# A linear-attention and feed-forward kernel: two prefetched weight pieces and eight small loads of the opening are put behind a GpSimd copy

## The chip, the core and the metric

The kernel runs on one core of one Trainium2 chip. Its time is the device time of one launch in microseconds (us). Three runs of the kernel before gave 631.48, 631.27 and 630.54 us, with a median of 631.27 us.

The core has five engines that work side by side, each through its own list of instructions in order: TensorE (PE in the profile; its weight loads are shown apart as PEld), VectorE (DVE), ScalarE (ACT), GpSimd (POOL) and SyncE (SP). SP computes nothing here. It issues DMA transfers from DRAM into the on-chip memory, one after the other, and an instruction of SP that has to wait holds up every transfer behind it.

## What is computed

The first half is a delta rule, a linear attention with a state that is corrected step by step, for 4 batches of 8 heads, 768 positions and 48 dimensions a head. The second half is a feed-forward layer with a leaky ReLU whose slope differs from unit to unit, on 3072 tokens of 384 features, with 2048 hidden units.

```python
k_n = k / (norm(k) + 1e-6)
for t in range(768):
    y[t]  = q[t] @ state
    v_old = state.T @ k_n[t]
    state = state + beta[t] * outer(k_n[t], v[t] - v_old)
x = y as (tokens, 8 heads * 48)
h = x @ w_in
g = max(h, 0) + alpha * min(h, 0)
out = g @ w_out
```

## The kernel before, in words

The sequence is cut into 12 chunks of 64 positions, and a chunk into two steps of two batches each, so there are 24 steps, numbered from 0. Steps 0 and 1 are the first chunk. Within a chunk the recurrence is a triangular system, and a step solves it with small matmuls: three rounds of substitution (lines 719 to 757), and then `solve` (line 907), whose result, `u`, VectorE takes out of PSUM with one instruction (line 914). From `u` come the step's outputs (line 923), and the state for the next chunk (line 942). Two steps make one chunk of 256 tokens for the feed-forward layer.

All instructions stand in the order in which the Python code emits them; no scheduler moves them. While the attention is a chain of small dependent matmuls, feed-forward matmuls (line 1088) are woven between them so that TensorE has work. The opening has no such work yet: `first_chunk` (line 1630) runs the three rounds for steps 0 and 1 in turn (line 732), with transposes of keys 4, 5 and 6 between them (line 430), then the two solves, the outputs, and the first feed-forward input (`to_ffn`). After it `second_pair` (line 1857) does steps 2 and 3 with the first feed-forward matmuls between.

The weights of the first layer, `w_in`, come in 12 pieces of 512 KB. A piece is fetched by one DMA into a staging place (line 246), rewritten there by two ScalarE instructions (lines 262 and 263, the function `begin`), and finished by two VectorE instructions (lines 272 and 277, the function `finish`). Pieces 0 to 5 and 8 to 11 are staged in the place that `w_out` will take later. Pieces 6 and 7 are staged in `space_out` (the trace names them by that tile). `spare_words` is a view of that tile, and the gates `beta` lie in its first words until they have been transposed. In ScalarE's list the two instructions for piece 6 and the two for piece 7 stand right behind the two copies of `to_ffn` for the first chunk (line 993), and ahead of the first ReLU of the feed-forward layer (line 1098).

Queries, keys and values come as 96 KB transfers (line 169), two to a step, each of 512 rows of 192 bytes, and the keys once more in another layout, as `kl`, in four transfers of 48 KB a step (line 197). These go through SP, in the order in which the code calls `load_early`, `load_q`, `load_v`, `load_late` and `fetch_in`. Eight semaphores are used for them in turn, so a transfer is issued only once the transfer eight places before it has landed.

In the opening SP's order is: keys, `beta`, values and queries of the first steps, weight pieces 0 to 5, then

```
weight pieces 6 and 7            fetch_in(n_in + 2), n_in = 6
keys 4, 5, 6                     load_early
kl of step 1                     load_late(1)
values 2, queries 2, queries 3   load_v, load_q
key 7                            load_early(NJ + NKE), NJ + NKE = 7
weight pieces 8 and 9            fetch_in(n_in + 4)
kl of step 2, values 3, ...      second_pair
```

Key 7 takes the place of key 4, and queries 2 and 3 those of queries 0 and 1, so they wait for the transposes of these; pieces 8 and 9 take the places of pieces 0 and 2 once VectorE has finished with them.

Of the kernel before, what the change touches and what calls it, by code (L numbers as in the profile page):

```python
# [25 lines left out]
FP32 = mybir.dt.float32  # L26
# [18 lines left out]
def kernel(  # L45
# [11 lines left out]
    nc = tc.nc  # L57
# [24 lines left out]
    def ps_one():  # L82
        return ps_big()[:, 0]
# [21 lines left out]
    def half(i):  # L105
        return slice(64 * i, 64 * i + 64)
# [17 lines left out]
    NKE, NKL, NQ = 3, 2, 2  # L124
# [11 lines left out]
    def early(n):  # L136

        if n >= TURNED_K:
            return k_last
        return k_late[1] if n == NKE else k_early[n % NKE]  # L140

    def fetch_blocks(src, c, first, dst):

        src = src.rearrange("b (g a) s d -> a (b g) s d", a=2)
        n = dst.shape[2]
        for i in range(2):
            at = c * C + HB * i
            for a in range(2):
                for e in range(2):
                    w = min(HB, D - HB * e)  # L150
                    x = src[a, first : first + n, at : at + HB, HB * e : HB * e + w]
                    rows = slice(64 * a + HB * e, 64 * a + HB * e + HB)
                    nc.sync.dma_start(
                        out=dst[rows, i, :, 0:w], in_=x.rearrange("x s d -> s x d")
                    )

    def blocks_of(x):
        return x.rearrange("p (i x e) -> p i x e", i=2, e=HB)
# [6 lines left out]
    def fetch(a, n, dst, queues=(nc.sync, nc.sync)):  # L165
        c, bp = steps[n]
        for t in range(2):
            src = a[2 * bp + t, :, c * C : (c + 1) * C, :].rearrange("h p d -> p h d")
            queues[t].dma_start(out=dst[half(t)], in_=src)

    def load_early(n, *queues):
        if n < N:
            fetch(k, n, early(n)[:, :, 0:D], *queues)

    def load_q(n):
        if TURNED_Q <= n < N:
            c, bp = steps[n]
            x = q_pad[n % NQ].rearrange("p h d -> p (h d)")
            fetch_blocks(q, c, 2 * bp * H // 2, blocks_of(x))
        elif n < N:  # L180
            fetch(q, n, q_pad[n % NQ][:, :, 0:D])

    def load_v(n):
        if n < N:
            v_raw[n] = work.tile([128, H, D], FP32, name="v_raw", bufs=3)
            fetch(v, n, v_raw[n])
# [113 lines left out]
    for t in range(2):  # L300
# [5 lines left out]
        out=ones, in_=ones, compare_op=ALU.is_ge, fill=1.0, base=0,  # L306
# [7 lines left out]
    for t in range(2):  # L314
# [5 lines left out]
        out=first_of, in_=ident.rearrange("p (q u e) -> p u q e", u=2, e=HB // 2)[:, 0],  # L320
# [162 lines left out]
    def quarters():  # L483
        return [(g, a, t) for g in range(G) for a in range(2) for t in range(2)]

    def now(pieces):
        for x in pieces:
            x()

    def region(p, n, **into):  # L490

        p = ps_big()[:, :, 0:n] if p is None else p
        assert p.shape[-1] == n
        return p.rearrange("p a (g i) -> p a g i", **into)
# [34 lines left out]
    NJ = 4  # L529
# [139 lines left out]
    def off_products(both):  # L669

        x = [act[:, FP - 4 + i].rearrange("p f i -> p (f i)") for i in both]
        x = [y.rearrange("p (h c) -> p h c", h=H) for y in x]
        for i in both:
            own = turned[0][:, i * H : i * H + H]
            nc.scalar.mul(x[i][:, :, 0:HB], own, which[:, 0:1])
            nc.vector.tensor_scalar_mul(x[i][:, :, HB:C], own, which[:, 1:2])
        n = C - LB
        own, other = [ps_big(), None], ps_big()
        own[1] = ps_big()
        for i in both:  # L680
            p = own[i][:, 0, 0 : H * n].rearrange("p (b i) -> p b i", b=H)
            q = (other[:, 0] if i == 0 else own[1][:, 1])[:, 0 : G * n]
            q = q.rearrange("p (b i) -> p b i", b=G)
            for b in range(H):
                for t in range(2):
                    w, y = x[i][half(t), b], mid[i][half(t), b, LB:C]
                    nc.tensor.matmul(p[half(t), b], w, y)
                    if b >= G:
                        nc.tensor.matmul(q[half(1 - t), b - G], w, y)
            nc.scalar.copy(diag[i][:, :, LB:C], p)  # L690
            other_.append(q)
        return [
            lambda i=i: nc.vector.tensor_copy(out=away[i][:, :, LB:C], in_=other_[i])
            for i in both
        ]
# [23 lines left out]
    def substitute(n, x, k, p=None):  # L719

        p = region(p, G * D, g=G)
        for g, a, t in quarters():
            frm, to, m, y = half(t), half(t), diag[n % NE][:, a * G + g], x[:, a, g]
            if a == 0:
                pass
            elif k % 2 == (1 if n < 2 else 0):
                to = half(1 - t)
            else:
                frm, m = half(1 - t), away[n % NE][:, g]
                if k == 0:  # L730
                    y = crossed[n][:, g]
            nc.tensor.matmul(p[to, a, g], m[frm], y[frm])
        return p
# [22 lines left out]
    def place_inverse(n):  # L756

        for i in range(2):
            nc.scalar.mul(
                inv[n % NE][:, :, HB * i : HB * i + HB], inverse[0][:, n * H : n * H + H],  # L760
                which[:, i : i + 1],
            )
# [88 lines left out]
    nv, rhs_, ys, us, xts, whole = {}, {}, {}, {}, {}, set()  # L851
# [55 lines left out]
    def solve(n, p=None):  # L907
        p = region(p, G * D, g=G)
        for g, a, t in quarters():
            nc.tensor.matmul(  # L910
                p[half(t ^ a), a, g], inv[n % NE][half(t), a * G + g], rhs_[n][half(t), a, g]
            )
        us[n] = work.tile([128, 2, G, D], FP32, name="u")
        return [lambda: nc.vector.tensor_tensor(  # L914
            out=us[n], in0=p,
            in1=stats[n][1][:, 0:3:2, :, None].to_broadcast([128, 2, G, D]), op=ALU.mult,
        )]
# [712 lines left out]
    def first_chunk(mask, inverted, convert):  # L1630

        both = (0, 1)
        ahead[0] = n_in
        aways = off_products(both)
        for _ in range(PIECES - 1):
            next(inverted)
        aways[0]()
        next(inverted)
        assert next(inverted, None) is None
        aways[1]()  # L1640
        place_inverse(0)
        now_at = {}
        for i in both:
            now_at[i] = rhs_[i]
        for k in range(3):
            for i in both:
                p = substitute(i, now_at[i], k)
                if k == 0:
                    now_at[i] = work.tile([128, 2, G, D], FP32, name="r")
                substituted(i, now_at[i], p, k)  # L1650
                if i == 0 and k < 2:
                    now(flipped(NJ + k, ps_one()))
                if (k, i) == (1, 0):
                    place_inverse(1)
                if (k, i) == (0, 1):
                    place(0, (3,))
                    for j in (3, 2):
                        off_blocks(j, by_pool=True)
                if (k, i) == (1, 1):
                    place(1, (3,))  # L1660
                    begin_in(6)
                if i == 0 and k > 0:
                    mask(0, k - 1)
        for i in both:
            squared(NJ + i)
        for i in both:
            rhs_[i] = now_at[i]
        weighted = solve(0)
        keys = flipped(NJ + 2, ps_one())
        now(weighted)  # L1670
        for a in range(2):
            mask(1, a)
        now(keys)
        now(solve(1))
        convert(6)
        for i in both:
            now(outputs(i))
        load_early(NJ + NKE)
        fetch_in(n_in + 4)
        for i in both:  # L1680
            to_ffn(i, ps_ffn())
        norms(NJ)
        ahead[0] = FT * DM
        convert(4)
        norms(NJ + 1)
# [26 lines left out]
    n_in = FT * DM // n  # L1712
    stages = [space[:, i * n : (i + 1) * n] for i in range(n_in)]
    spare_words = space_out.rearrange("p s e -> p (s e)")
    stages += [spare_words[:, i * n : (i + 1) * n] for i in range(2)]
    ids = [*range(n_in + 2), 0, 2, 1, 3]
    fetch_in, begin_in, conv_in = weights(pieces, stages, ids, in_done, n_in + 2)
# [89 lines left out]
    gram_3 = gram(3)  # L1807
    turned_beta = big[1]
    later_signs = betas(1, NCH // 2, turned_beta[:, 1, G * C :])
    fetch_in(n_in + 2)  # L1810
    cross(0)
    nc.scalar.copy(inside, ones)
    now(gram_2[2:])
# [3 lines left out]
    edges(0, edge)  # L1817
    cross(1)
    load_late(1)
    load_v(2)  # L1820
    for i in range(2):
        flips(N, i)
    for i in range(2):
        load_q(i + 2)
    mask = queries()
    for i in range(2):
        off_blocks(i)
# [15 lines left out]
    def convert(n):  # L1843
        for _ in part(conv_in, n):
            pass
# [294 lines left out]
```

## Time and profile before

| | |
|---|---|
| three runs, median | 631.27 us (630.54 to 631.48) |
| the profiled execution's own time | 632.44 us |
| its span, first to last instruction | 630.7 us |
| granted TensorE clock, mean | 0.997 |
| PE busy | 617.4 us, 98% of the span |
| DVE, ACT, POOL busy | 504.0, 312.4, 99.9 us |
| moved by DMA | 39.26 MB, mean 62 GB/s |

In the profile, a row of the timeline gives the start and the length in us, the engine, the source line, what the instruction writes and reads with its shape, and in brackets how long the engine had been idle before it, and what ended that. "<-issue" means that nothing the profile shows was waited for. A row of busy times by stretch gives, for the stretch named first, its length, then the busy time and the number of instructions of PE, PEld, DVE, ACT and POOL, the granted TensorE clock, the mean busy share of the 16 DMA engines, and GB/s. A row of DMA issues gives what is written and read, the queue, the number, the size of one in KB, and the median us from issue to landing. Rows of DMA queues give packets, MB, and busy time as a share of 16 engines' time; the queue "q8 instruction" carries program code, not data.

Times in the text are us from the start of the span.

### The profile page before, as it was taken

Reading aid. Unit: us, or ns where it says so; the run is one execution under the profiler, and the core shown is the slowest. Engines: PE = TensorE matmul, PEld = TensorE weight load, DVE = VectorE, ACT = ScalarE, POOL = GpSimd, SP = SyncE. Lnnn points to the kernel's source line nnn. Section 1 sums busy time; section 2 is a strip of 40 time slices with the busy share of each in tenths; the row PEclk is TensorE's granted clock in tenths of the full one; section 3 lists DMA queues with packets and bytes.
Section 4 is the critical chain, followed back from the end, with each engine's and each line's share of the span. In section 5 each row is a group of like instructions: output and inputs, shape, how many; then the busy total and the mean of one; then the engine's idle time right before and its main releaser. Section 6 shows DMA issues by size and latency. Waiting matters only on the chain.

```text
span 630.7 us, 21675 instructions
## 1 busy us (share of the span) xinstructions
PE 617.4 (98%) x9116; PEld 545.5 (86%) x9116; DVE 504.0 (80%) x1223; ACT 312.4 (50%) x836; POOL 99.9 (16%) x218
## 2 busy tenths in 40 slices
PE   6989999999999999999999999999999999999997
PEld 5678788566789989989989989989999999999997
DVE  5978999979989988968978868878979579386383
ACT  6878566255544256446345446335356366352230
POOL 7032221010001000000000000000053062061350
PEclk9989999999999999999999999999999999999999
DMA  7958845212252241241341121211220300100100
GB/s 117 301 120 193 242 87 161 41 38 51 44 85 44 56 73 27 54 74 30 51 76 30 39 40 27 53 26 27 46 51 13 62 15 11 30 3 1 26 1 25
DMA packets 145968, 39.26 MB, mean 62 GB/s; under 512 B 139040, under 2 KB 142256, under 8 KB 145872
## 3 DMA queue, kind: packets, MB, share of 16 engines
q1 hardware_dynamic: 144000, 37.40, 29.0%
q8 instruction: 71, 1.16, 0.7%
q10 hardware_dynamic: 1872, 0.49, 0.4%
q14 instruction: 25, 0.20, 0.1%
HBM read 33.14 MB, written 4.72 MB: 60 GB/s over the span
## 4 chain that ended last, share of the span: by engine, by line
PE 87%; DVE 5%; ACT 3%; DMA 2%; issue 1%; SPq 1%; ACTq 0%; DVEq 0%
PE p_ffn L1088 16%; PE p_ffn L1152 10%; PE p_more L1088 8%; PE p_more L1422 8%; PE p_more L1152 8%; PE p_ffn L1131 5%; PE p_more L1338 5%; PE p_ffn L1328 3%; PE p_ffn L1422 3%; PE p_ffn L1333 3%; PE p_pair L885 2%; PE p_pair L923 2%; PE p_pair L809 2%; PE p_pair L910 2%; PE p_pair L502 2%; PE p_pair L867 2%
## 5 line engine op out<-in xcount | busy, mean ns | idle before, releaser
L1088 PE MATMUL p_ffn<-xt,w_in 128*128 128x256 f32 x528 | 123.2, 384 | 0.1
L1088 PEld LDWEIGHTS p_ffn<-xt,w_in 128*128 128x128 f32 x528 | 97.6, 190 | 14.1 <-issue 0.4
L979 ACT COPY xt<-z 32x96 f32<-32x96 f32 x240 | 64.5, 269 | 49.4 <-DVE z L966 46.3
L1088 PE MATMUL p_more<-xt,w_in 128*128 128x256 f32 x240 | 55.7, 382 | 0.0
L1362 POOL TENSOR_TENSOR k_t<-k_t 128x128 f32<-128x128 f32 (+1 forms) x48 | 28.3, 591 | 166.3 <-ACT k_t L1357 163.8
L600 DVE TENSOR_TENSOR block<-block,prod 128x30 f32<-128x30 f32 (+9 forms) x150 | 50.0, 333 | 5.1
L1088 PEld LDWEIGHTS p_more<-xt,w_in 128*128 128x128 f32 x240 | 44.9, 190 | 6.3
L594 DVE TENSOR_TENSOR prod<-block 128x30 f32<-128x30 f32 (+9 forms) x150 | 48.6, 324 | 1.3
L419 POOL TENSOR_TENSOR beta_t<-beta_t,rec 128x8 f32<-128x8 f32 x24 | 6.9, 288 | 231.8 <-DVE rec L413 228.0
L1100 DVE SCALAR_TENSOR_TENSOR act<-act,al_t,p_ffn 128x256 f32<-128x256 f32 x72 | 31.0, 471 | 14.5 <-ACT act L1098 14.4
L826 ACT COPY inv<-p_pair 32x256 f32<-32x256 f32 x30 | 10.9, 363 | 59.2 <-DVE u L914 35.5
L1098 ACT ACTIVATE act<-p_ffn 128x512 f32<-128x512 f32 x36 | 21.4, 594 | 22.7 <-PE p_ffn L1088 22.4
L1362 POOL TENSOR_TENSOR block<-block 128x128 f32<-128x128 f32 (+1 forms) x48 | 27.7, 577 | 12.6 <-ACT block L1357 10.1
L1328 PE MATMUL p_ffn<-xt,w_in 128*128 128x256 f32 x96 | 29.3, 387 | 0.0
L1152 PE MATMUL p_ffn<-w_out,act 128*128 128x192 f32 x160 | 27.7, 327 | 0.0
L914 DVE TENSOR_TENSOR u<-p_pair,wgt 128x384 f32<-128x384 f32 x24 | 13.2, 554 | 16.8 <-PE p_pair L910 9.9
L1152 PEld LDWEIGHTS p_ffn<-w_out,act 128*128 128x128 f32 x160 | 26.2, 190 | 0.3
L1100 DVE SCALAR_TENSOR_TENSOR act<-act,al_t,p_more 128x256 f32<-128x256 f32 x40 | 17.3, 474 | 10.9 <-ACT act L1098 10.7
L895 DVE TENSOR_TENSOR r<-v_raw,p_pair 64x192 f32<-64x192 f32 (+1 forms) x66 | 23.2, 352 | 2.1 <-PE p_pair L885 1.0
L1152 PE MATMUL p_more<-w_out,act 128*128 128x192 f32 x128 | 22.3, 326 | 0.0
L1357 ACT COPY k_t<-p_more 128x512 f32<-128x512 f32 x16 | 9.4, 587 | 25.5 <-PE p_more L1338 18.9
L1422 PE MATMUL p_more<-w_out,act 128*128 128x192 f32 x128 | 21.6, 327 | 0.0
(285 smaller groups left out, 1486.5 us busy)
## 6 DMA issues: line engine op xcount, KB each, us to landing
w_out<-in_moe_w_in_dram SPq DMA_DIRECT2D x10, 512.0 KB, 5.6
v_raw<-in_v_dram SPq DMA_DIRECT2D x48, 96.0 KB, 2.9
kl<-in_k_dram SPq DMA_DIRECT2D x96, 48.0 KB, 2.4
out_dram<-o_sb SPq DMA_DIRECT2D x90, 48.0 KB, 1.6
space_out<-in_moe_w_out_dram SPq DMA_DIRECT2D x11, 384.0 KB, 4.0
ke_last<-in_k_dram SPq DMA_DIRECT2D x25, 96.0 KB, 3.5
qp<-in_q_dram SPq DMA_DIRECT2D x64, 32.0 KB, 2.2
w_out<-in_moe_w_out_dram SPq DMA_DIRECT2D x5, 384.0 KB, 5.3
```

Of the source, the lines that this page charges most:

```text
L594: nc.vector.tensor_tensor(out=prod, in0=r[:, 0:j, j : j + 1].to_broadcast([128, j, n]), in1=r[:, j : j + 1, j + 1 : HB].to_broadcast([128, ...
L600: nc.vector.tensor_tensor(out=r[:, 0:j, j + 1 : HB], in0=r[:, 0:j, j + 1 : HB], in1=prod, op=ALU.add)
L895: nc.vector.tensor_tensor(out=r[to, a], in0=v_in[to, a], in1=p[own, a, :, 0:D], op=ALU.subtract)
L979: nc.scalar.copy(to[quad(r), u, bp, t], z[quad(2 * t + u), r])
L1088: nc.tensor.matmul(p_h[:, i], w_in[:, t, (f + i) * 128 : (f + i + 1) * 128], xt[:, t], start=(t == 0), stop=(t == KT - 1),)
L1100: nc.vector.scalar_tensor_tensor(out=g[:, i], in0=g[:, i], scalar=al_t[:, f + i : f + i + 1], in1=p_h[:, i], op0=ALU.mult, op1=ALU.add,)
L1131: nc.tensor.matmul(p_o[u], gs[f // 2][:, f % 2, u * 128 : (u + 1) * 128], w_out[:, f], start=(f == 0), stop=(f == FT - 1),)
L1152: nc.tensor.matmul(p, x(i), w(i), start=(i == 0), stop=(i == FP - 1))
L1328: nc.tensor.matmul(p[:, f * 256 : f * 256 + 256], w(2, f), xt[:, 2], start=True, stop=False)
L1338: nc.tensor.matmul(q[:, j], a, b, start=True, stop=True)
L1362: nc.gpsimd.tensor_tensor(out=dst, in0=a, in1=b, op=ALU.add)
L1422: nc.tensor.matmul(p, x(i), w(i), start=(i == 0), stop=(i == FP - 1))
```

## The change

In `first_chunk`, behind the second `solve`, GpSimd gets one more instruction: it copies one word of step 1's `u` into the first word of `spare_words`, the place where piece 6 is staged. The transfer of piece 6 writes that word too, so SP must wait for the copy, and everything behind it on SP waits as well. The fetch of pieces 6 and 7 moves from its place behind the gates to here, and so do the loads of queries 2 and 3 and values 2; key 7, which was called a few lines further down, stands among them. The order on SP between `kl` of step 1 and weight pieces 8 and 9 becomes: piece 6, queries 2, key 7, piece 7, queries 3, values 2. Ten transfers are moved, 1792 KB in all. The lists of PE, DVE and ACT keep their order; POOL's has the one copy more, between the blocks of line 667 and the copies of line 709.

```diff
@@ first_chunk
         now(keys)
         now(solve(1))
+        held_back = spare_words[0:1, 0:1].bitcast(FP32)
+        nc.gpsimd.tensor_copy(out=held_back, in_=us[1][0:1, 0, 0, 0:1])
+        fetch_in(n_in + 1)
+        load_q(2)
+        load_early(NJ + NKE)
+        fetch_in(n_in + 2)
+        load_q(3)
+        load_v(2)
         convert(6)
         for i in both:
             now(outputs(i))
-        load_early(NJ + NKE)
         fetch_in(n_in + 4)
@@ the opening
     later_signs = betas(1, NCH // 2, turned_beta[:, 1, G * C :])
-    fetch_in(n_in + 2)
     cross(0)
@@
     cross(1)
     load_late(1)
-    load_v(2)
     for i in range(2):
         flips(N, i)
-    for i in range(2):
-        load_q(i + 2)
     mask = queries()
```

## The prediction

> **What bounds the kernel now.** I read the page, the chain of waits, and then the opening in the timeline, in stretches and in its DMA. PE is busy for 98% of the span; the chain is 87% PE and from 75 us on nearly all PE. What is lost before that is not made up later, so a shift at 50 us is a shift of the end. In the opening PE isn't full:
>
> ```profile
> q1 hardware_dynamic: 144000, 37.40, 29.0%
> q8 instruction: 71, 1.16, 0.7%
> ...
> 34.10 0.55 PE L732 MATMUL p_pair<-r,diag 64*64 64x48 f32 x21
> 36.41 0.39 PE L732 MATMUL p_pair<-r,diag 64*64 64x48 f32 x12 [1.77 <-issue]
> ...
> q8 instruction: 1, 0.02, 3.0%
> ...
> 30.06:33.48 3.42, 3.42 (x170) 3.13 (x162) 2.57 (x7) 2.50 (x7) 1.84 (x3) 1.00 0.70 109
> 33.48:36.89 3.41, 1.64 (x65) 1.31 (x60) 1.13 (x5) 2.69 (x8) 2.97 (x6) 1.00 0.54 98
> 36.89:40.30 3.41, 3.41 (x94) 3.14 (x86) 2.80 (x7) 1.47 (x3) 0.00 (x0) 0.50 0.62 115
> 40.30:43.71 3.41, 2.92 (x108) 2.25 (x106) 2.89 (x7) 2.00 (x4) 0.00 (x0) 1.00 0.38 68
> ```
>
> PE stops for 1.77 us in the middle of one group of matmuls (round two, step 1), where no wait stands. The code queue q8 carries PE's program: 1.16 MB in 71 packets is 16 KB each, and over PE's 9116 matmuls and 9116 weight loads 64 bytes an instruction, so 256 a packet. One packet (the single one in the DMA between 33 and 35 us) moves from 34.1 to 35.0, and PE goes on at 36.41. I read the gap as PE out of program. The block it ran out of was entered 256 instructions earlier, near 31.1; if the next is asked for then, its packet started some 3 us late, while key transfers were queued. The next packet starts at 37.6, only 1.2 us after the crossing at 36.41, with shorter queues. Second, the granted clock changes at 36.89 and 40.30, so I cut stretches of that length: after the one with PE busy for 1.64 of 3.41 us it is 0.50 for the next 3.41 us; after 2.92 of 3.41 it stays 1.00.
>
> Behind this stage the limit is ScalarE's list, nearly full from 50 to 62 us:
>
> ```profile
> 43.80 0.48 ACT L993 COPY xt<-p_ffn 128x384 f32<-128x384 f32 x1 [0.18 <-PE p_ffn L991]
> 44.17 0.69 ACT L262 ACTIVATE w_in<-space_out 128x512 uint32<-128x512 uint32 x1
> 45.47 0.68 ACT L262 ACTIVATE w_in<-space_out 128x512 uint32<-128x512 uint32 x1
> 46.17 0.69 ACT L263 ACTIVATE space_out<-space_out 128x512 f32<-128x512 f32 x1
> 48.03 0.60 ACT L1098 ACTIVATE act<-p_ffn 128x512 f32<-128x512 f32 x1 [1.17 <-PE p_ffn L1088]
> 49.86 0.59 ACT L456 COPY k_t<-p_pair 112x512 f32<-112x512 f32 x1 [0.48 <-PE p_pair L430]
> ...
> space_out<-in_moe_w_in_dram SPq DMA_DIRECT2D x2, 512.0 KB, 11.7
> ...
> w_out<-in_moe_w_in_dram SPq DMA_DIRECT2D x1, 512.0 KB, 3.8
> ...
> space_out<-in_moe_w_out_dram SPq DMA_DIRECT2D x1, 384.0 KB, 4.2
> ```
>
> Pieces 6 and 7 are on chip long before ScalarE reaches them (44.17, 45.47). It idles for 1.17, then 0.27 and 0.48 us up to 49.86; from there to 55.0, where PE waits for ScalarE's copy of line 458, there is no slack. The DMA rows are pieces 6 and 7 in the queue; a 512 KB piece issued alone at 42.88; and a 384 KB piece behind four 96 KB loads, at 58.11.
>
> **The change, part by part.** The sum is made on the profiled execution: span 630.7, own time 632.44, against a median of 631.27. I take differences and subtract them from the median.
>
> *Taken away before 38 us.* 1.05 MB less goes ahead of keys 4 to 6. At the 391 GB/s that the DMA moves between 22 and 25 us that is 2.7 us, and SP issues a transfer only when the eighth before it has landed, so keys and `kl` of step 1 are issued and land about 2.7 us sooner. Before, keys landed until 33.3 us; then until about 30.6. Values 2, queries 2 and 3 and key 7 are gone from 33.7 to 40.4. At 31.1 little but `kl` is queued. With the 1.2 us of the later packet the code packet starts at 32.3, and with the 2.35 us from its start at 34.06 to PE's going on at 36.41 PE could go on at 34.65: when it ran dry. I take the whole 1.77 us; bounds 0 and 1.77.
>
> *The clock.* Without the gap the stretch from 33.48 would be mostly busy, and I expect no drop. At 0.50 the rest of rounds two and three took 2.13 us for 73 matmuls, where 64 take 1.15 to 1.28 at full clock (69.3 and 60.0 us); the solve 1.14 against 0.66; the transposes of key 6 1.05 against 0.65. Excess 0.75 + 0.48 + 0.40 = 1.6, less 0.2 that VectorE's own steps keep: 1.4, bounds 0 and 1.7. So step 1's `u`, done at 41.80 before, would be done at 41.8 - 1.8 - 1.4 = 38.6.
>
> *Added: the wait.* GpSimd is idle there for 12.8 us (36.7 to 49.5), so its copy delays nobody but SP. No row has a copy of one word; the smallest GpSimd copy (64x64, line 301) takes 0.23 us and the smallest instruction 0.10. With VectorE's signal to it and its own to SP I take 0.3, bounds 0.1 and 0.5. SP starts at 38.9. Piece 6 takes 0.45 to issue (0.43 to 0.5 in its rows), lands at 38.9 + 3.8 = 42.7, and ScalarE wants it at 44.17 - 3.2 = 41.0. Then queries 2 and key 7, four issues of 0.64 (two in 1.27): piece 7 is issued at 41.9. The rows for landing run from 3.8 (512 KB, alone) over 4.2 (384 KB behind four small loads) to 6.2 (the same behind two, at 65.26). I take 4.2, the nearest in place: 46.1. From there ScalarE needs two instructions of 0.70, the ReLU 0.6 and line 707's copy 0.4: it reaches line 456 at 48.45, against 49.86. The gain is 1.4 instead of 3.2: the wait costs 1.8. Everything from line 456 on follows ScalarE, and then VectorE and PE in their old distances.
>
> *The others behind SP.* Queries 2 and key 7 land by 44.6 (2.9 after the last issue) and are wanted at 48.74 - 3.2 = 45.5: hidden by 0.9. Queries 3 are out by 43.6 and land at 46.6, wanted at 48.7. Values 2 are issued by 44.9 and land near 48, wanted by VectorE at 53.5. Pieces 8 and 9, issued at 44.9 and 45.4, land near 49 and 51 and are wanted by ScalarE at 51.60 - 1.4 and 55.55 - 1.4: covered by about 1 and 3 us. After that SP has its old order at about its old absolute time. Keys 4 to 6 sooner gain nothing by themselves: PE's transposes at 31.88 and 33.52 did not wait.
>
> Sum: -1.77 - 1.4 + 1.8 = -1.4 us, **629.9 us**. Its own range is -2.4 (landing 3.8, small clock loss) to -0.2 (landing 5.4, as the 512 KB piece issued at 45.02).
>
> A rule that speaks against it: after a stretch with 1.64 of 3.41 us busy the next shows 0.50. The Trainium skill's "TensorE: Matmul & The Clock Gate" (Part 1: The HAM clock gate) has the clock drop after an idle window of about 3.4 us; no such window is here, so by it the drop has another cause, the 1.4 us would not come back, and the time would be 631.3. The rows show the drop in the next such window, so I go by them.
>
> **The rivals.**
>
> *Starvation stays (slower).* The gap is not due to the queued data, or is met again one block on, where PE at full clock eats 256 instructions in 2.5 us. Then `u` stays at 41.8, piece 7 is issued at 45.1, lands at 49.3, and line 456 is reached at 51.65: +1.8 us, **633.1**. For it: a packet needs 2.35 us from start to effect even in a quiet queue. Against it: PE had the next packets in time under traffic. It decides as soon as less than 1.8 of the 3.2 us comes back.
> The Trainium skill's "Runtime: NRT & Kernel Launch" (Instruction fetch mechanics) says that the next 16 KB block is fetched while the present one runs and that crossing is mostly hidden; by it this rival holds. The block size agrees with q8's packets; the idle 1.77 us does not look hidden.
>
> *ScalarE stands longer at piece 7.* Its landing is worth its delay one for one. Broken even at 5.6 us after issue; 6.2 gives +0.6, 7.5 gives +1.9. For it: the row of 11.7 for these very pieces, and 6.2 behind only two small loads at 65.26; against it: at most five transfers stand ahead of piece 7, one of them large. I price it at 7.0, between 6.2 and the 9.3 of the key loads that stood behind pieces 6 and 7: +1.4, **632.7**.
>
> *Piece 7 is hidden.* If it lands within 3 us, or ScalarE's slack takes it, the gain is 2.6 to 3.2: 628.4. Against it: no 512 KB row is under 3.8.
>
> **How the numbers follow.** A measurement of this kernel tells 0.2% (1.26 us) from no change. Forecast 0.50 (0.32 below -1.26, 0.18 within); starvation 0.20 (0.19 slower, 0.01 within); ScalarE longer 0.20 (0.12 slower, 0.08 within); hidden 0.10 (faster). Faster 0.42, same 0.27, slower 0.31. The range from 628.5 to 633.2 takes in the forecast's own and both slower rivals' values, and leaves out about 0.15: the best of the hidden case and the worst of the slower ones.
>
> **What the profile after would show.** No PE idle of over 0.5 us inside line 732's group at 34 to 37 us; granted clock 1.00 from 33 to 44; step 1's `u` (second row of line 914) ending near 38.6; SP's first row behind `kl` at 38.9; ScalarE idle ahead of line 262 on `space_out` for 1.5 us, then 2 us; line 456 on ScalarE near 48.5. I am wrong if the gap stands or moves by one block, if the clock drops in another stretch, or if line 456 isn't earlier.

## The result: 0.9% slower, and the profile after

Five runs of the changed kernel have a median of 636.65 us (635.09 to 638.24), against 631.27 before: a ratio of 1.009, with a 95% interval of 1.0069 to 1.0111. The prediction was 629.9, and its range ended at 633.2. The profiled execution took 636.65 us, with a span of 634.9.

Busy times by stretch, the first two rows of the kernel before, the last two of the changed kernel:

```profile
33.00:40.00 7.00, 5.23 (x176) 4.79 (x168) 3.92 (x10) 4.61 (x12) 3.38 (x7) 0.78 0.57 103
40.00:54.00 14.00, 13.51 (x335) 10.91 (x334) 12.83 (x28) 10.16 (x21) 2.25 (x5) 0.99 0.64 143
```

```profile
33.00:40.00 7.00, 5.42 (x219) 4.49 (x211) 4.79 (x13) 4.94 (x13) 3.06 (x7) 1.00 0.02 5
40.00:54.00 14.00, 11.13 (x264) 8.95 (x265) 9.99 (x21) 6.68 (x13) 0.99 (x3) 1.00 0.93 211
```

The last three numbers of a row are the clock, the DMA engines' busy share and GB/s. The clock stays at 1.00, as forecast. But the DMA engines, busy for 0.57 of the time from 33 to 40 us before, now stand still there, and from 40 to 54 us they are full (0.93). In that stretch PE loses 2.4 us (13.51 to 11.13).

PE's stops, in the timeline of the changed kernel:

```profile
33.78 0.55 PE L732 MATMUL p_pair<-r,diag 64*64 64x48 f32 x21
35.28 0.39 PE L732 MATMUL p_pair<-r,diag 64*64 64x48 f32 x12 [0.95 <-issue]
39.01 0.45 PE L910 MATMUL p_pair<-r,inv 64*64 64x48 f32 x16 [0.48 <-issue]
48.53 0.62 PE L430 MATMUL p_pair<-ident,ke_pair 128*112 128x128 f32 x4 [1.36 <-DMA ke_pair<-in_k_dram]
```

The stop for program code is 0.95 us at the same instruction where it was 1.77, and a second one of 0.48 us follows 256 PE instructions later. New is a wait for key 7. ScalarE's list, first of before (the piece behind key 7's copies, and a `w_out` piece), then of the changed kernel:

```profile
51.60 0.66 ACT L262 ACTIVATE w_in<-w_out 128x512 uint32<-128x512 uint32 x1
73.70 0.57 ACT L262 ACTIVATE w_out<-w_out 128x384 uint32<-128x384 uint32 x1 [0.96 <-DMA w_out<-in_moe_w_out_dram]
```

```profile
45.01 0.68 ACT L262 ACTIVATE w_in<-space_out 128x512 uint32<-128x512 uint32 x1 [2.38 <-DMA space_out<-in_moe_w_in_dram]
50.53 0.66 ACT L262 ACTIVATE w_in<-space_out 128x512 uint32<-128x512 uint32 x1 [4.13 <-DMA space_out<-in_moe_w_in_dram]
52.63 0.60 ACT L456 COPY k_t<-p_pair 112x512 f32<-112x512 f32 x1
54.38 0.66 ACT L262 ACTIVATE w_in<-w_out 128x512 uint32<-128x512 uint32 x1
79.00 0.57 ACT L262 ACTIVATE w_out<-w_out 128x384 uint32<-128x384 uint32 x1 [2.38 <-DMA w_out<-in_moe_w_out_dram]
```

ScalarE stands 2.38 us for piece 6 and 4.13 us for piece 7, reaches line 456 at 52.63 (49.86 before) and piece 8 at 54.38 (51.60 before). Much later it stands again, for a piece of `w_out`. Three rows of the DMA issues of the changed kernel between 40 and 50 us, with the median us from issue to landing last:

```profile
space_out<-in_moe_w_in_dram SPq DMA_DIRECT2D x2, 512.0 KB, 5.5
w_out<-in_moe_w_in_dram SPq DMA_DIRECT2D x2, 512.0 KB, 5.8
ke_pair<-in_k_dram SPq DMA_DIRECT2D x2, 96.0 KB, 5.1
```

Piece 6 leaves at 40.55 and lands 4.4 us later; piece 7 leaves at 43.94 and takes 6.57 us; key 7 takes 5.13 us. Pieces 8 and 9 leave at 48.46 and 49.67, where they left at 42.88 and 45.02.

**One way to read the span.** In all profiles below the span splits into three parts: the end of step 1's `u` (second row of line 914); from there to ScalarE's first instruction for piece 8 (line 262, behind key 7's copies); and the rest. Before: 41.80 + 9.80 + 579.1 = 630.7. After: 40.15 + 14.23 + 580.5 = 634.9.

### The profile page after: what moved, and what is told of

Same layout as the page of the kernel before. It is cut to its first block, busy times and chain, and to the rows that moved or that the text cites. A ratio compares the mean times of both kernels' runs of the same rounds, so it can differ in the third digit from the quotient of the medians.

```text
span 634.9 us, 21676 instructions
## 1 busy us (share of the span) xinstructions
PE 618.3 (97%) x9116; PEld 545.0 (86%) x9116; DVE 503.6 (79%) x1223; ACT 312.5 (49%) x836; POOL 99.8 (16%) x219
## 4 chain that ended last, share of the span: by engine, by line
PE 86%; DVE 4%; ACT 3%; DMA 3%; SPq 2%; issue 1%; ACTq 0%; DVEq 0%
PE p_ffn L1088 16%; PE p_ffn L1152 10%; PE p_more L1088 8%; PE p_more L1422 8%; PE p_more L1152 8%; PE p_ffn L1131 5%; PE p_more L1338 5%; PE p_ffn L1328 3%; PE p_ffn L1422 3%; PE p_ffn L1333 3%; PE p_pair L885 2%; PE p_pair L923 2%; PE p_pair L809 2%; DMA ke_pair<-in_k_dram 2%; PE p_pair L910 2%; PE p_pair L867 2%
## 5 line engine op out<-in xcount | busy, mean ns | idle before, releaser
L1152 PE MATMUL p_more<-w_out,act 128*128 128x192 f32 x128 | 22.3, 326 | 0.0
L885 PE MATMUL p_pair<-beside,k_t 48*64 48x112 f32 x704 | 21.4, 259 | 0.4 <-ACT beside L458 0.2
```

Of the source, the lines that this page charges most:

```text
L885: nc.tensor.matmul(p[half(t ^ a), a, g], k_t[n][dims(a), g, half(t)], beside[bp][dims(a), t, g])
L1152: nc.tensor.matmul(p, x(i), w(i), start=(i == 0), stop=(i == FP - 1))
```

## The experiments

Four theories were put against each other. One: ScalarE, which works in order, stands at piece 7. Two: PE waits for the late small loads, key 7 above all. Three: holding itself costs, since whatever leaves behind `u` comes too late. Four, formed after the first four runs: SP's list, some 5 us longer behind the hold, makes all that follows late.

The parts of the span, in us, with the ratio to the kernel before and its 95% interval:

| kernel | ratio | `u` done | `u` to line 456 | `u` to piece 8 | rest |
|---|---|---|---|---|---|
| before | 1 | 41.80 | 8.06 | 9.80 | 579.1 |
| before_again | 1 | 38.80 | 8.07 | 9.81 | 582.4 |
| before_once_more | 1 | 39.02 | 8.07 | 9.81 | 584.1 |
| weights_mid | 1.0009 (0.9987 to 1.0031) | 40.13 | 8.06 | 9.80 | 579.1 |
| weights_held | 0.9999 (0.998 to 1.0018) | 38.86 | 9.22 | 10.98 | 579.1 |
| no_hold | 1.0009 (0.9982 to 1.0036) | 42.67 | 9.14 | 10.88 | 581.1 |
| loads_held | 1.0035 (1.0013 to 1.0057) | 40.39 | 8.15 | 11.58 | 580.6 |
| before_lag | 1.004 (1.0023 to 1.0057) | 39.12 | 8.07 | 14.65 | 580.4 |
| four_held | 1.0044 (1.0019 to 1.0068) | 39.62 | 10.15 | 11.90 | 580.4 |
| half_held | 1.0049 (1.0032 to 1.0067) | 40.77 | 11.67 | 13.42 | 579.1 |
| key_free | 1.0062 (1.004 to 1.0084) | 38.94 | 10.66 | 14.00 | 580.0 |
| weights_first | 1.008 (1.0055 to 1.0106) | 38.64 | 10.33 | 14.05 | 579.7 |
| after | 1.009 (1.0069 to 1.0111) | 40.15 | 12.48 | 14.23 | 580.5 |
| after_again | as after | 39.16 | 12.68 | 14.43 | 581.3 |
| after_defer | 1.0091 (1.0055 to 1.0127) | 41.20 | 9.56 | 13.81 | 581.2 |
| by_pool | 1.0105 (1.008 to 1.0131) | 39.24 | 14.14 | 15.88 | 580.3 |

The times of one kernel scatter by several us (before: 629.5 to 636.5 over the runs beside these), so the ratios go by all runs of a kernel and of the kernel before beside it, and the parts are of one execution each.

### Was the stop before a fixed thing? before_again, before_once_more, after_again

These are the two kernels, unchanged.

> The kernel before, unchanged, for a second look at the stop at 34.65 to 36.41 us and at the clock. If the stop is fixed by the data that is queued at 31 us, PE stops again at the same instruction for 1.5 to 2.1 us, with half a clock behind it. If it is a matter of chance from one execution to the next, its length differs by a microsecond or more.

> The same once more: with a fixed stop 1.5 to 2.1 us; with chance, anything from 0 to 3 us, and the start of step 1's solve scattered as much.

> The changed kernel, unchanged, for a second look. If the order sets it, piece 7 lands 6 to 7 us after its issue and ScalarE stands 4 us ahead of it, PE about 1.4 us for key 7, and the stops for code are 0.95 us or less. If chance had a hand in it, piece 7's landing differs by over a microsecond.

Measured: 632.78, 634.62 and 636.64 us. First the stretch of the old stop in before_again, then what PE did there later on:

```profile
33.48:36.89 3.41, 3.31 (x139) 2.98 (x136) 3.15 (x10) 2.66 (x7) 2.73 (x6) 1.00 0.48 79
```

```profile
70.39 0.35 PE L502 MATMUL p_pair<-k_t 48*64 48x64 f32 x9 [2.30 <-issue]
```

And the same place in before_once_more:

```profile
71.12 0.49 PE L502 MATMUL p_pair<-k_t 48*64 48x64 f32 x9 [2.79 <-issue]
```

In the stretch from 33.48, where PE was busy for 1.64 us in the first profile, it is busy for 3.31 and 3.34 us in these two. The stop of 1.77 us isn't there, nor the half clock behind it, and `u` is done at 38.80 and 39.02 instead of 41.80. Both executions stop elsewhere instead, for 2.30 and 2.79 us at 68 us, and the half clock comes there, from 70.89 and 70.32 on. That is where their longer rests come from, 582.4 and 584.1 us; the first profile of before (579.1) and both of the changed kernel have no such stop and no half clock behind piece 8. From 30 to 80 us all stops of over 0.4 us that wait for nothing the profile shows stand at a PE instruction number of 193 or 194 + 256k, in every profile that has one, as the ends of blocks of program code would; which of these crossings catches PE, and for how long, differs from one execution to the next. The changed kernel's second look repeats the first: piece 7 lands 6.53 us after its issue, ScalarE stands 4.04 us for it.

The mean of `u` over the five profiles in which pieces 6 and 7 go ahead of keys 4 to 6 (before three times, loads_held, before_lag) is 39.83; over the ten in which they don't (no_hold left out, whose piece 6 leaves just as PE crosses; 39.94 with it) it is 39.67. Single values run from 38.64 to 41.80, so 0.16 us between the means is no difference, and a gain of 3.2 us isn't there. By that spread a gain of a microsecond or so can't be ruled out (an estimate).

### Which of the held transfers cost? weights_held, loads_held, weights_first, no_hold

```diff
 weights_held, against before: only pieces 6 and 7 behind the hold; others in their old order
         now(solve(1))
+        load_early(NJ + NKE)
+        held_back = ...; nc.gpsimd.tensor_copy(...)
+        fetch_in(n_in + 2)
     ...
-        load_early(NJ + NKE)
     ...
-    fetch_in(n_in + 2)
 loads_held, against before: only the small loads, held by a word of queries 2; their old calls go
+        held_back = q_pad[2 % NQ][0:1, 0, 0:1]; nc.gpsimd.tensor_copy(...)
+        load_q(2); load_early(NJ + NKE); load_q(3); load_v(2)
 weights_first, against the changed kernel
-        fetch_in(n_in + 1); load_q(2); load_early(NJ + NKE); fetch_in(n_in + 2)
+        fetch_in(n_in + 2); load_q(2); load_early(NJ + NKE)
 no_hold, against the changed kernel
-        held_back = ...; nc.gpsimd.tensor_copy(...)
```

> Only weight pieces 6 and 7 are held back; values 2, queries 2 and 3 and key 7 keep their places behind kl of step 1. Theory one (ScalarE's list stands at piece 7, whose landing is late because four small loads are issued ahead of it and share the DMA with it): piece 7 is now issued 0.45 us behind piece 6, at about 41 to 42.5, and lands by 46 to 47.5 instead of 50.5; ScalarE reaches line 456 at 48.5 to 50 instead of 52.6, and SP has no backlog behind piece 7; 629.5 to 632. Theory two (the late small loads, key 7 above all, are what costs): 631 or less as well, since they land by 43. Theory three (the holding itself costs, since any landing behind 40.5 is too late for ScalarE): the time stays above 634.

> Only the eight small loads are held back (GpSimd's word goes into the place of queries 2); weight pieces 6 and 7 are fetched ahead as before. Theory one: ScalarE finds pieces 6 and 7 at 44 and 45.5 and doesn't stand; key 7, issued at 42 to 43.5, lands by 47 and is wanted at about 48, so line 456 is reached near 50; what is left is SP's backlog of 8 issues of 0.64 us, 5 us for pieces 8 and 9 and all behind; 631 to 633. Theory two: PE waits for key 7 as in the changed kernel; 634 to 637.

> All is held, but pieces 6 and 7 are issued first and the small loads behind them. Theory one: piece 7 is issued near 41 and lands by 46.5, and ScalarE is past it at about 48; key 7 is issued some 0.6 us later than in the changed kernel and lands near 49, so line 456 comes near 51; with SP's backlog as it was, 633 to 635. Theory two: key 7 is later still and the time is 636.6 or more.

> The new order on SP without GpSimd's copy: pieces 6 and 7 and the small loads are issued as soon as their places are free, from about 30.7 us on. Nothing is late for ScalarE or PE. If the starvation of program code at 34 to 36 us and the clock's drop are due to data that is queued with the code packet, they return, and the time is 630.5 to 632; if they are due to the data ahead of keys 4 to 6 alone, or to nothing of the data, PE stops for 1.4 us in two places as in the changed kernel, the clock stays at 1.00, and the time is 629 to 630.3.

Measured medians: 631.66, 634.36, 636.1 and 632.59, with 631.57 for before beside them. So holding the two weight pieces costs nothing that can be measured (its interval ends at 0.18%, 1.1 us, and the profile has piece 8 1.2 us later behind `u`), and theory three falls for them. ScalarE in weights_held:

```profile
44.66 0.67 ACT L262 ACTIVATE w_in<-space_out 128x512 uint32<-128x512 uint32 x1 [3.31 <-DMA space_out<-in_moe_w_in_dram]
45.94 0.69 ACT L262 ACTIVATE w_in<-space_out 128x512 uint32<-128x512 uint32 x1
48.08 0.61 ACT L456 COPY k_t<-p_pair 112x512 f32<-112x512 f32 x1
```

Piece 7 lands 1.3 us behind piece 6 when it is issued right behind it. The small loads held alone cost 0.35%, though line 456 isn't late by them. Loads_held, ScalarE:

```profile
48.54 0.59 ACT L456 COPY k_t<-p_pair 112x512 f32<-112x512 f32 x1 [0.51 <-PE p_pair L430]
51.97 0.67 ACT L262 ACTIVATE w_in<-w_out 128x512 uint32<-128x512 uint32 x1 [1.60 <-DMA w_out<-in_moe_w_in_dram]
76.60 0.55 ACT L262 ACTIVATE w_out<-w_out 128x384 uint32<-128x384 uint32 x1 [1.46 <-DMA w_out<-in_moe_w_out_dram]
```

It stands for piece 8, which left at 47.22 (42.88 before), and again for `w_out`. Theory one, as it stood, doesn't explain this run; theory four came out of it. Weights_first came out between the two ranges expected. There piece 7 is nearly on time, but now PE waits 2.23 us for key 7, whose halves land at 47.27 and 47.74, and piece 8 comes as late as in the changed kernel:

```profile
47.88 0.62 PE L430 MATMUL p_pair<-ident,ke_pair 128*112 128x128 f32 x4 [2.23 <-DVE w_in L277]
48.97 0.58 ACT L456 COPY k_t<-p_pair 112x512 f32<-112x512 f32 x1 [2.15 <-PE p_pair L430]
```

(The profile names VectorE as PE's releaser, whose instruction of line 277 ends at 47.84. But line 430 transposes key 7, and PE starts 0.14 us after its landing here, as it does in the changed kernel, where the profile names the DMA. So key 7 is the likelier cause; it isn't shown.) No_hold was expected to give 629 to 630.3, or 630.5 to 632 with the stop; its median of 632.59 is 0.09% over before, no difference. Its profile is of an execution of 636.34 us, with a stop of 3.12 us at the known instruction: piece 6 left at 30.23, and PE crossed into a new block at 30.49.

### SP's list alone, half of it, another queue, no hold: before_lag, half_held, by_pool, weights_mid

```diff
 before_lag, against before
         load_early(NJ + NKE)
+        for e in range(4):
+            for t in range(2):
+                src = q[t, :, e * C : (e + 1) * C, :].rearrange("h p d -> p h d")
+                nc.sync.dma_start(out=idle[half(t), e], in_=src[:, :, 0:1])
         fetch_in(n_in + 4)
 half_held, against the changed kernel: out of the hold, to their old places
-        load_q(3); load_v(2)
 by_pool, against the changed kernel: small loads issued by GpSimd
-        load_q(2); load_early(NJ + NKE); ...; load_q(3); load_v(2)
+        load_q(2, nc.gpsimd); load_early(NJ + NKE, (nc.gpsimd, nc.gpsimd)); ...
+        load_q(3, nc.gpsimd); load_v(2, nc.gpsimd)
 weights_mid, against before
-    fetch_in(n_in + 2)
     ...
     for i in range(2):
         load_q(i + 2)
+    fetch_in(n_in + 2)
```

> The kernel before, with eight further DMAs on SP ahead of weight pieces 8 and 9: each has 512 rows as a small load has, but of 4 bytes, so SP's list gets about 5 us longer and next to no data moves. Nothing else is changed: pieces 6 and 7, key 7, queries and values are fetched as before. Theory four (after loads_held, where line 456 was early and the time was still 2.8 us up: SP's list, 5 us behind, makes pieces 8 to 11 and the first pieces of w_out late, and PE waits at 73 to 80 us): 633 to 635, with ScalarE idle ahead of line 262 on w_out's pieces. Theory one (what costs is ScalarE standing at piece 7): 631 to 632.

> Queries 3 and values 2 go back to their old places ahead of the hold; piece 6, queries 2, key 7 and piece 7 stay held, in this order. Theory four: SP's backlog falls from 8 issues to 4, so pieces 8 and 9 are issued near 44.5 instead of 48.4, the w_out pieces 2.5 us sooner, and the time is 633 to 634.5. Theory one: piece 7 is issued and lands as in the changed kernel, line 456 stays at 52 and the time at 636 to 637.

> The changed kernel, but the eight small loads are issued by GpSimd, behind its copy, and SP has only pieces 6 and 7 to hold, then 8 and 9. The loads are as late as in the changed kernel, SP has no backlog and piece 7 is issued behind piece 6. Theory four and theory one together: 631 to 633. If the lateness of key 7 and queries 2 is what costs (theory two): 634 to 636.5.

> No hold: pieces 6 and 7 stand behind queries 3, ahead of key 7, and so leave at about 36 and land by 41. ScalarE then doesn't stand at all, as before; keys 4 to 6 come early, as in the changed kernel. If program code is late by the data that is queued when PE crosses into a new block, PE has no stop at 34 us, and one of 1 to 2 us near 38, with a half clock behind it in some runs; 630 to 631.5. Without such a stop 628.5 to 629.5.

Measured medians: 634.43, 634.71, 638.24 and 632.02. Before_lag moves 2 KB a transfer and holds nothing, and it costs 0.4% (0.23 to 0.57), some 2.5 us. Its lines are numbered one higher. ScalarE, then PE:

```profile
47.19 0.59 ACT L457 COPY k_t<-p_pair 112x512 f32<-112x512 f32 x1 [0.48 <-PE p_pair L431]
53.77 0.66 ACT L263 ACTIVATE w_in<-w_out 128x512 uint32<-128x512 uint32 x1 [4.75 <-DMA w_out<-in_moe_w_in_dram]
```

```profile
55.53 1.00 PE L886 MATMUL p_pair<-beside,k_t 48*64 48x112 f32 x32 [3.09 <-ACT diag L708]
```

Line 456 (here 457) is 8.07 us behind `u`, as before; then ScalarE stands 4.75 us for piece 8, and PE 3.09 us for the copy that stands behind it. So eight issues too many ahead of pieces 8 and 9 are enough for a loss, with no weight piece late but these. Half_held, with four issues taken out of the hold, regains 1.9 us of the 5.4 and lands where theory four put it, though slightly above its range. Its profile doesn't bear theory four out: piece 8 landed at 51.58, long before ScalarE came to it at 54.19. ScalarE stands for piece 7 instead, and so reaches line 456 11.67 us behind `u`:

```profile
50.34 0.67 ACT L262 ACTIVATE w_in<-space_out 128x512 uint32<-128x512 uint32 x1 [3.27 <-DMA space_out<-in_moe_w_in_dram]
```

By_pool was to show that SP's list is all. It misses that, 631 to 633, by 5 us, and lies above theory two's range as well. SP issues pieces 6 to 9 at 39.64, 40.02, 40.95 and 42.53, with no backlog, yet they land at 43.80, 47.07, 50.53 and 54.39, and PE stands:

```profile
51.41 1.07 PE L430 MATMUL p_pair<-ident,ke_pair 128*112 128x128 f32 x4 [5.16 <-DMA ke_pair<-in_k_dram]
```

```profile
40.00:54.00 14.00, 8.73 (x163) 7.03 (x158) 9.29 (x19) 5.61 (x11) 6.26 (x10) 0.88 1.00 220
```

The second row is its stretch from 40 to 54 us: the DMA engines are busy all the time. From the first issue to the last landing, the four pieces and eight small loads (2.9 MB) take 15.4 us here (39.56 to 54.99) and 15.2 us (40.55 to 55.76) in the changed kernel. Two queues don't make them faster. The Trainium skill's "DMA: Bandwidth & Descriptors" (Issuing engines are not separate DMA queues) says so: issuing from several engines saves only the issuing time. This run agrees with it. So theory four is half of it: behind the hold SP's list is too long, and the DMA engines are full as well; whichever transfer stands last in the order is late.

In weights_mid the two pieces leave at 34.77 and 35.44, ahead of key 7, land by 41.50, and nothing is late: `u` to piece 8 is 9.80, as before. Its time is no different from before (0.09% over), and above both ranges expected. So clearing the pieces out of the stretch ahead of keys 4 to 6, with nothing late behind it, gains nothing that can be measured.

### Key 7 ahead of the hold: key_free

```diff
 key_free, against the changed kernel
+        load_early(NJ + NKE)
         held_back = ...; nc.gpsimd.tensor_copy(...)
-        fetch_in(n_in + 1); load_q(2); load_early(NJ + NKE); fetch_in(n_in + 2)
+        fetch_in(n_in + 2); load_q(2)
         load_q(3); load_v(2)
```

> As weights_first, but key 7 is issued ahead of the hold: held are pieces 6 and 7, then queries 2 and 3 and values 2. If two prices add up in weights_first, SP's backlog (8 issues, about 2.9 us by before_lag) and PE's stop for key 7 (2.2 us), only the first is left, with 6 issues: 633.3 to 634.7. If key 7's lateness costs nothing beside the backlog, 635.5 or more; if it was all, 631 to 632.

The median is 634.89, with 632.11 for before beside it, some 1.2 us below weights_first by the medians and 0.2 above the range, and the two intervals overlap. Key 7 now lands by 41.63, but piece 6 takes 6.1 us, PE waits 1.87 us for queries 2, and piece 8 stays at 14.00 behind `u`. That prices add up is not shown by it: as one late transfer is mended, the next stands in its place.

### ScalarE's order, and a sum: after_defer, four_held

```diff
 after_defer, against the changed kernel: ScalarE's two instructions for piece 7 later
-        ahead[0] = FT * DM          # first_chunk
+        ahead[0] = FT * DM          # second_pair, behind flips(x + 3, n)
 four_held, against the changed kernel: key 7 ahead of the hold, queries 2 in their old place
+        load_early(NJ + NKE)
         held_back = ...; nc.gpsimd.tensor_copy(...)
-        fetch_in(n_in + 1); load_q(2); load_early(NJ + NKE); fetch_in(n_in + 2)
+        fetch_in(n_in + 2)
         load_q(3); load_v(2)
     ...
+    load_q(2)
```

> The changed kernel with one thing moved: ScalarE's two instructions for piece 7 stand behind its copies of key 7 (lines 456, 458) instead of ahead of the first ReLU. SP's order, the hold and every landing stay. If ScalarE standing 4 us for piece 7 is what puts line 456 at 12.6 us behind u (8.1 before), it now comes 10 to 11 us behind u, as soon as key 7 has landed, and the time falls by 1 to 2.5 us, to 634 to 635.7. If key 7 or SP's backlog holds it anyway, line 456 stays 12 us or more behind u and the time at 636 to 637.

> Queries 2 and key 7 go back ahead of the hold; held are pieces 6 and 7 in a row, then queries 3 and values 2. If the cost is the sum of a late piece 7, a late key 7 and SP's backlog, line 456 comes about 9 to 9.5 us behind u (as in weights_held), the backlog is 4 issues, about 1.3 us, and the time is 632 to 633.5. If the backlog doesn't add up like that: below 632 or above 634.

After_defer has a median of 637.53, no faster than the changed kernel and above both ranges. Its ScalarE:

```profile
50.76 0.59 ACT L456 COPY k_t<-p_pair 112x512 f32<-112x512 f32 x1 [1.97 <-PE p_pair L430]
52.50 0.66 ACT L262 ACTIVATE w_in<-space_out 128x512 uint32<-128x512 uint32 x1
55.01 0.67 ACT L262 ACTIVATE w_in<-w_out 128x512 uint32<-128x512 uint32 x1 [1.14 <-DMA w_out<-in_moe_w_in_dram]
```

Line 456 does come 9.56 us behind `u` instead of 12.5, as the first half of the expectation had it. But of these 3 us only 0.4 to 0.6 are left at piece 8: it landed at 54.99, and ScalarE stands for it. In the changed kernel piece 8 had landed at 53.93, as far behind `u` as here (13.8 us), and ScalarE was free for it at 54.38. There the wait for piece 7 covers the wait for piece 8, half a microsecond apart, so taking away the first alone gains nothing. Theory one alone falls by this. Theory four alone falls by half_held, where piece 7 sets the delay and piece 8 doesn't, and by weights_first, where line 456 is late with piece 7 nearly on time.

Four_held has a median of 633.7, 0.44% over before, 0.2 us above its range. Line 456 comes 10.15 us behind `u` (9 to 9.5 expected), ScalarE doesn't stand for piece 8, and the rest is 1.3 us longer than 579.1, as expected for four issues. Half_held, also with four, has 579.1; why is open. Of the 1.3 us, 0.66 are a wait of PE at 73 us that half_held doesn't have.

## Why the prediction was wrong

**The 1.77 us gap (first term).** The reading of the row was right, PE was out of program, and the block of 256 instructions holds in every profile. What failed is that one execution's stop was taken as a property of the kernel. Two further executions of the kernel before have no stop there. In the changed kernel's two profiles the stops at these two crossings are 0.95 and 0.48 us, and one of 0.48 us; the DMA was idle at both of 0.48, and the packet for the one of 0.95 left at 33.03, when the last `kl` had landed (32.84). Of the 3.2 us that this term and the next forecast together, 0.2 us are left on the means of `u` above. The rival "starvation stays" was right that PE at full speed meets the next block: 256 instructions later it stops for 0.48 us. Its rule, from the Trainium skill's "Runtime: NRT & Kernel Launch" (Instruction fetch mechanics), that a crossing is mostly hidden, held at this crossing in two executions of three, and didn't at 68 us.

**The clock (second term).** With the stop gone the clock stays at 1.00 here, as forecast, but the 1.4 us were part of the same chance. The reading of the rows itself was borne out in part. Windows of 3.41 us of no_hold and before_lag, each pair the window and the next one:

```profile
34.62:38.03 3.41, 0.89 (x43) 0.77 (x42) 0.42 (x2) 2.99 (x8) 1.31 (x3) 1.00 0.08 10
38.03:41.45 3.42, 3.35 (x79) 2.94 (x80) 2.72 (x7) 0.15 (x1) 0.00 (x0) 0.50 0.59 102
```

```profile
53.08:56.49 3.41, 0.96 (x44) 0.96 (x48) 0.00 (x0) 2.68 (x6) 0.68 (x2) 1.00 1.08 224
56.49:59.90 3.41, 3.41 (x101) 3.19 (x91) 2.21 (x7) 2.84 (x8) 0.00 (x0) 0.50 0.63 150
```

After windows with PE busy for 0.89 and 0.96 us the next is at half clock, and in no_hold again after one with 2.13 us (58.52 to 61.94); none was idle as a whole. But the busy time alone doesn't settle it: in the changed kernel PE is busy for 2.06 us from 46.42 to 49.84, and the next window stays at 1.00. The Trainium skill's "TensorE: Matmul & The Clock Gate" (Part 1: The HAM clock gate) asks for an idle window; the measurement decides for partly idle ones.

**The wait (third term, +1.8).** SP started 0.40 us behind `u` (0.3 forecast). The failing step is the landing of piece 7: 4.2 us was taken, the nearest row in place, and 6.57 and 6.53 were measured. That nearest row came from a DMA that had other work behind it; here ten transfers leave in one burst, with pieces 8 and 9 behind them. With 0.4 us more of issuing, line 456 came 12.5 us behind `u` against 9.85 in the forecast. The rival "ScalarE stands longer" had the mechanism, and its 7.0 was near; its time was 632.7, since it too counted on the 3.2 us.

**The others behind SP.** "Hidden by 0.9" failed for key 7: 5.13 us to land where 2.9 was taken, and PE waited 1.36 us. "After that SP has its old order at about its old absolute time" is the step that cost most beside the first: pieces 8 and 9 left 5.6 and 4.6 us later than before and took 5.5 and 6.1 us. Before_lag prices such a lag by itself at some 2.5 us, and after_defer shows it standing right behind piece 7's.

**The sum, redone.** From 629.9: 3.0 us for a gain that isn't there (3.2 less 0.2), 2.7 for line 456 (12.5 against 9.85), 1.4 for the longer rest (580.5 against 579.1) give 637.0, against 636.65 measured. This is an estimate: the parts come from single executions. The last term is the least certain, though no stop for code and no half clock stands in either of these rests, and the second look has 581.3.

**What would have shown it.** The forecast's own list did: the gap was "no PE idle of over 0.5 us" (0.95 and 0.48), `u` near 38.6 (40.15), SP at 38.9 (40.55), ScalarE standing 1.5 and 2 us (2.38 and 4.13), line 456 near 48.5 (52.63). Only the clock came as written.

**Open.** What makes a code packet late at one crossing and not at the next isn't settled. No version was found that beats the kernel before: weights_held and weights_mid can't be told from it.

## What to carry to other kernels

Before a stop or a clock drop in one profile is counted as a gain, look at a second execution of the same kernel: here it was chance. Transfers that are taken out of a stretch in which the DMA engines are half idle and put behind a wait leave in one burst. Two weight pieces alone could be moved so at no measurable cost; all ten couldn't. So price the last of the burst, and those behind it on the same queue, at the burst's rate and not at the landing time of a lone transfer. When an in-order list stands at one late input, ask what it would find at the next: a wait can cover another that ends at nearly the same time, and then removing the first alone gains nothing.

## What the runs showed of the hardware

- Behind a crossing into a new code block at 34 to 35 us, with the DMA nearly idle (after, after_again, weights_first), the next packet starts after 1.1 us and moves for 1.2 us, and PE goes on in the block behind 1.4 us after that: 3.7 us in all. PE works through the block between in 3.0 us (34.28 to 37.31 in after_again), so even a quiet queue leaves a stop, of 0.48 us in these three. The block ahead of it takes 3.3 to 3.4 us (30.49 to 33.79 in weights_first, 30.89 to 34.31 in before_again).
- The 96 KB loads of 192-byte rows fill the DMA engines at some 180 GB/s (an estimate from 103 GB/s at a share of 0.57, before, 33 to 40 us); 512 KB pieces alone land 1.3 us apart, near 400 GB/s (pieces 6 and 7 in weights_held).
- A DMA of 512 rows of 4 bytes holds SP for about as long as one of 512 rows of 192 bytes: eight of them took it from 41.34 to 47.78 in before_lag, some 0.63 us each and one pause of 0.9 us.
